# Moving the exponents ahead of two turns, and half-loads of q, in a chunked mLSTM recurrence

## The chip, the cores and the metric

The kernel runs on one core of one Trainium2 chip. The metric is the device time in microseconds of one execution. A core has five engines that run side by side, each through its own list of instructions in order: TensorE (PE) multiplies matrices and turns (transposes) tiles, its weight loads are shown as PEld; VectorE (DVE) and ScalarE (ACT) work elementwise; GpSimd (POOL) works elementwise[...]; SyncE (SP) issues transfers. TensorE writes only to PSUM, a small memory, from which VectorE or ScalarE copy. A buffer may be written again only when its last reader has ended, and this kernel fixes the order of every engine's list by the order of its source.

## What is computed

Two parts. The first is an mLSTM cell: for each of 4 batches and 8 heads, over 768 positions with 40 numbers each,

```python
for t in range(S):
    m_new  = np.maximum(f_gate[:, :, t] + m, i_gate[:, :, t])
    f_stab = np.exp(f_gate[:, :, t] + m - m_new)
    i_stab = np.exp(i_gate[:, :, t] - m_new)
    m = m_new
    C = f_stab * C + i_stab * einsum('bhd,bhe->bhde', vt, kt)
    n = f_stab * n + i_stab * kt
    h_tilde = einsum('bhde,bhe->bhd', C, qt)
    denom = np.maximum(np.abs(einsum('bhd,bhd->bh', n, qt)), 1.0)
    y[:, :, t] = sigmoid(o_gate[:, :, t]) * h_tilde / denom
```

The second takes the result as 3072 rows of 320 numbers. Each row goes by a hash of its token to one of 8 experts, `out = relu(x @ w1[e]) @ w2[e]`, with 1024 hidden numbers. The change touches the first part alone.

## The kernel before

The recurrence is done in chunks of 128 positions: 4 batches of 6 chunks are 24 steps (`NT`), step `s` being chunk `c = s % 6` of batch `b = s // 6`. Inside a chunk the recurrence is a masked, decay-weighted attention; between chunks a state C is carried. The step of the loop works on several chunks at once: it turns k for step s+2, makes the decay weights, scores and weighted scores for step s+1, attends for step s, and turns and stores the output of step s-1.

Names in the profile: `kT`, `qT` are turned k and q; `ab` the exponents' arguments, `w` the exponents (and later the weighted scores); `xb` the decay of the carried state, spread over partitions, read by `qs` (q times decay) and by `dec` (decay of the whole chunk); `ht` the output, turned, with the state's update (from `kw`) beside it in the same tile; `hT` its copy; `xo` the output turned back; `sp` scores; `R` the decay rows of a chunk; `ql` q of a whole batch as loaded, `qp` one sixth of it, padded; `og` the output gates; `tk` a small table for the experts.

```python
def load_q(b):                       # 960 KB: all heads of a batch
    qb[b] = {"l": ld.tile([P, H, NB * D], F32, name="ql", bufs=2)}
    nc.sync.dma_start(qb[b]["l"][:], q[b].rearrange("h (p r) d -> p h (r d)", r=NB))

def turn_k(s):
    d["kT"] = wk.tile([P, PR, P], F32, name="kT")
    tp = ps.tile([P, PR, P], F32, name="tr", tag="tr", bufs=2)
    for j in range(PR):              # PR = 4
        nc.tensor.transpose(tp[:, j, :], d["k"][:, 2 * j : 2 * j + 2, :]..., ident[:])
    nc.scalar.copy(d["kT"][:], tp[:])

def pad_q(b, r):
    t = qb[b][r] = qps[2 + r % 2]
    nc.vector.tensor_copy(t[:, :, :D], qb[b]["l"][:, :, r * D : (r + 1) * D])

def turn_q(b, r, cols):              # cols: every sixth position, from r
    t = qb[b].pop(r)
    tp = ps.tile([P, PR, P], F32, name="tr", tag="tr", bufs=2)
    for j in range(PR):
        nc.tensor.transpose(tp[:, j, :], t[:, 2 * j : 2 * j + 2, :]..., ident[:])
    nc.scalar.copy(qb[b]["T"][:, :, cols], tp[:])

def decays(s):
    for hf in range(2):
        ab = ps.tile([P, PR, P], F32, name="ab", bufs=2)
        for i in range(2):
            nc.tensor.matmul(ab[i * HB : (i + 1) * HB], lhsT=Ls[b % 2][...], rhs=R[:, i, hf::2, :], ...)
        nc.scalar.activation(w[:, hf], ab[:], AF.Exp)
    if c > 0:
        xb = ps.tile([P, PR, P], F32, name="xb", tag="tr", bufs=2)
        ...                          # two matmuls
        nc.vector.tensor_tensor(d["qs"][:], q_of(s), xb[:], op=ALU.mult)
        nc.scalar.copy(d["dec"][:], xb[:, :, P - 1 :])

def back(s):
    xo = d["xo"] = ps.tile([P, 2, 2, P], F32, name="xo", tag="tr", bufs=2)
    ...                              # four transposes of hT

def finish(s):                       # VectorE and GpSimd: reads xo, divides, returns the store
    ...
```

One PSUM tag, "tr", with two buffers, serves `turn_k`, `turn_q`, `back`, `xb` and `tk` in turn. The loop:

```python
turns_of = {0: (0,), 1: (1, 2), 2: (3,), 3: (4,), 4: (5,)}          # which sixths of the next batch's q
first_turns = {1: (0,), 2: (1, 2), 3: (3,), 4: (4, 5)}              # the same in batch 0
for s in range(NT):
    b, c = s // NB, s % NB
    ...                              # loads of k, v (three steps ahead)
    if c == 5 and b + 2 < B:
        load_q(b + 2)
    ...                              # output gates, a slice of expert weights
    decayed(s)
    if s + 2 < NT:
        turn_k(s + 2)
    if b == 0 and c < 4:
        turn_q0(c + 2)               # batch 0's own q, loaded by chunks
    if b + 1 < B:
        for r in (turns_of if b else first_turns).get(c, ()):
            turn_q(b + 1, r, slice(r, None, NB))
    if s > 0:
        back(s - 1)
        store = finish(s - 1)
    if s + 1 < NT:
        decays(s + 1)
    if s + 2 < NT:
        load_a(s + 2, nc.scalar if s == 0 else nc.sync)    # R
    ...
    if s > 0 and (s, "all") in og:
        sigmoid(s)                   # steps 3, 9, 15, 21; step 0's stands at the step's end
    state(s)                         # C update
    ...
    if s > 0:
        store()
    if s + 1 < NT:
        scores(s + 1)
        weigh(s + 1)
    ...                              # pad_q for the turns of the next step
    attend(s)                        # C part, then v part, then hT
    ...                              # tk and other small pieces for the experts
```

Of the kernel before, what the change touches and what calls it, by code (L numbers as in the profile page):

```python
# [8 lines left out]
F32 = mybir.dt.float32  # L9
# [8 lines left out]
P = 128  # L18
# [4 lines left out]
def kernel(  # L23
# [24 lines left out]
    nc = tc.nc  # L48
    B, H, S, D = q.shape
    BH = B * H  # L50
    NB = S // P
# [4 lines left out]
    NT = N // P  # L56
    PR = H // 2
# [47 lines left out]
    def weight_slices(e):  # L105

        W[e], slices = weights(moe_w1[e], moe_w2[e], wpools[e % 3 // 2], w2pools[2 <= e < 6])
        return slices
# [8 lines left out]
    with tc.tile_pool(name="gates", bufs=1) as gp, \  # L117
# [35 lines left out]
        qb = {}  # L153
# [5 lines left out]
        def load_k(s):  # L159
            st[s] = {"k": ks[s % NK], "v": vs[s % NK]}  # L160
            nc.sync.dma_start(ks[s % NK][:, :, :D], rows_of(k, s))

        def load_v(s):
            nc.sync.dma_start(vs[s % NK][:, :, :D], rows_of(v, s))
# [11 lines left out]
                        og[i] = tile_o[:, i - s0]  # L176
            nc.sync.dma_start(og[s], rows_of(o_gate, s))

        def load_q(b):

            qb[b] = {"l": ld.tile([P, H, NB * D], F32, name="ql", bufs=2)}
            nc.sync.dma_start(qb[b]["l"][:], q[b].rearrange("h (p r) d -> p h (r d)", r=NB))

        def load_e(b, gs):
            src = ze_d.rearrange("(g b h) i t -> b (h i) g t", g=NC2, h=H)[b]
# [5 lines left out]
        def load_a(s, eng):  # L191
            b, c = s // NB, s % NB
            r0 = c // 2 * BH + b * H
            n = 3 if c == 0 else 6
            src = za_d[r0 : r0 + H, :n, c % 2 * P : (c % 2 + 1) * P].rearrange("h i t -> i h t")
            for i in range(2):
                eng.dma_start(Rs[s % 2][32 : 32 + n, i], src)
# [59 lines left out]
        def gates_turn(rows):  # L257
            r = rows
            n = r.stop - r.start
            tp = ps.tile([P, 2, n], F32, name="tpg", tag="tr", bufs=2)  # L260
            for c in range(2):
                nc.tensor.transpose(tp[:, c, :], aP[r, c * P : (c + 1) * P], ident[r, r])
            lo, hi_ = (0, 1) if r.start == 0 else (1, 3)
            nc.vector.tensor_copy(
                kw_T[:, :, lo:hi_, :].rearrange("p c g n -> p c (g n)"), tp[:],
            )

        def turn_k(s):
            d = st[s]
# [3 lines that stand above are left out]
                nc.tensor.transpose(tp[:, j, :], d["k"][:, 2 * j : 2 * j + 2, :].rearrange("p h d -> p (h d)"), ident[:])  # L273
            nc.scalar.copy(d["kT"][:], tp[:])  # L274
# [15 lines left out]
        def load_q0(c):  # L290
            t = qb.setdefault(0, {})[c] = qps[c % 2]
            nc.sync.dma_start(t[:, :, :D], rows_of(q, c))

        def turn_q0(c):
            turn_q(0, c, slice(c * P, (c + 1) * P))

        def q_of(s):
            c = s % NB
            return qb[s // NB]["T"][:, :, c * P : (c + 1) * P]

        def decays(s):
            b, c = s // NB, s % NB
            d = st[s]
            R = Rs[s % 2]
            w = d["w"] = wk.tile([P, 2, PR, P], F32, name="w")
# [3 lines that stand above are left out]
                    nc.tensor.matmul(  # L309
                        ab[i * HB : (i + 1) * HB], lhsT=Ls[b % 2][:, c * P + i * HB : c * P + (i + 1) * HB],  # L310
                        rhs=R[:, i, hf::2, :], start=True, stop=True,
# [5 lines that stand above are left out]
                    nc.tensor.matmul(  # L317
                        xb[hf * DP : (hf + 1) * DP], lhsT=Lx[:], rhs=R[:, 0, hf::2, :], start=True, stop=True,
                    )
                d["qs"] = wk.tile([P, PR, P], F32, name="qs")  # L320
                nc.vector.tensor_tensor(d["qs"][:], q_of(s), xb[:], op=ALU.mult)
                d["dec"] = wk.tile([P, PR, 1], F32, name="dec")
                nc.scalar.copy(d["dec"][:], xb[:, :, P - 1 :])
# [89 lines left out]
        def back(s):  # L413
            d = st[s]
# [3 lines that stand above are left out]
                    nc.tensor.transpose(xo[:, hf, i, :], d["hT"][:, hf, i, :], ident[:])  # L418

        def finish(s):  # L420
            d = st.pop(s)
            hs = d["xo"].rearrange("p f i (x d) -> p f (i x) d", d=DP)
            den = wk.tile([P, 2, PR, 1], F32, name="den")
            nc.vector.tensor_scalar(
                den[:], hs[:, :, :, D:D1], scalar1=-1.0, scalar2=1.0, op0=ALU.mult, op1=ALU.max,
            )
            nc.vector.tensor_tensor(den[:], den[:], hs[:, :, :, D:D1], op=ALU.max)
            x = wk.tile([P, H, D], F32, name="x")
            xv = x.rearrange("p (j f) d -> p f j d", f=2)
            nc.vector.tensor_tensor(  # L430
                xv, hs[:, :, :, :D], og[s].rearrange("p (j f) d -> p f j d", f=2), op=ALU.mult,
            )
            nc.vector.reciprocal(den[:], den[:])  # L433
            nc.gpsimd.tensor_tensor(xv, xv, den[:].to_broadcast([P, 2, PR, D]), op=ALU.mult)  # L434
            return lambda: nc.sync.dma_start(x_d[s * P : (s + 1) * P, :], x.rearrange("p h d -> p (h d)"))
# [168 lines left out]
        after = {4: [route_counts], **{13 + i: [lambda i=i: route_table(i)] for i in range(NT // TH)}}  # L604
        after[12 + NT // TH].append(route_index)
        one = gp.tile([P, 2, 1], F32, name="one")
        turns_of = {0: (0,), 1: (1, 2), 2: (3,), 3: (4,), 4: (5,)}
        first_turns = {1: (0,), 2: (1, 2), 3: (3,), 4: (4, 5)}

        def tables():  # L610

# [76 lines left out]
        for t in vs:  # L688
            nc.gpsimd.memset(t[:, :, D1:], 0.0)
            nc.gpsimd.memset(t[:, :, D:D1], 1.0)  # L690
        load_q(1)
        gates_turn(g0)
        decays(0)
        load_a(1, A)
# [17 lines left out]
        slices = []  # L712
        for s in range(NT):
            b, c = s // NB, s % NB
            if 0 < s < NT - 3:
                load_k(s + 3)
                if b == 0 and c < 3:
                    load_q0(c + 3)
            if s + 3 < NT:
                load_v(s + 3)  # L720
            if c == 5 and b + 2 < B:
                load_q(b + 2)
            for i in range(2):
                o = s - (s - 3) % 6 + 6 + 2 * ((s - 3) % 6 - 1) + i if s > 2 else 3 + 2 * s + i
                if o < NT and (s < 3 or 1 <= (s - 3) % 6 <= 3):
                    load_o(o)
            if s in (3, 13):
                slices += weight_slices(s // 10)
            if slices:
                slices.pop(0)()  # L730
            decayed(s)
            if s + 2 < NT:
                turn_k(s + 2)
            if b == 0 and c < 4:
                turn_q0(c + 2)
            if b + 1 < B:
                for r in (turns_of if b else first_turns).get(c, ()):
                    turn_q(b + 1, r, slice(r, None, NB))
            if s > 0:
                back(s - 1)  # L740
                store = finish(s - 1)
            if s + 1 < NT:
                decays(s + 1)
            if s + 2 < NT:
                load_a(s + 2, nc.scalar if s == 0 else nc.sync)
            if s == 0:
                load_e(0, [1, 2])
            if c == 3 and b + 1 < B:
                load_e(b + 1, [0, 1, 2])
            if s > 0 and (s, "all") in og:  # L750
                sigmoid(s)
            state(s)
            if s + 1 < NT:
                k_weights(s + 1)
# [5 lines that stand above are left out]
            nb = b + (c == NB - 1)  # L760
            if nb + 1 < B and s + 1 < NT:
                for r in (turns_of if nb else first_turns).get((c + 1) % NB, ()):
                    pad_q(nb + 1, r)
            for piece in before.get(s, []):
                piece()
            attend(s)
            if s == 0:
                sigmoid(0)
                gates_turn(g1)
            for piece in after.get(s, []):  # L770
                piece()
# [92 lines left out]
    with tc.manual_schedule():  # L864
# [42 lines left out]
        for e in range(E):  # L907
# [3 lines left out]
            h = xp.tile([P, FB, CAP], F32, name="h")  # L911
# [23 lines left out]
    with tc.If(nx > 0):  # L935
        with tc.For_i(0, nx, 1) as k:
# [12 lines left out]
            h = xp.tile([P, FB, CAP], F32, name="h")  # L949
# [34 lines left out]
```

## Time and profile before

| | before |
|---|---|
| median of 3 runs | 448.51 us (447.72 to 449.46) |
| span of the profiled execution | 447.2 us |
| TensorE busy | 393.6 us (88%) |
| VectorE, ScalarE, GpSimd busy | 134.9, 136.3, 118.5 us |
| first step's kT turn / last stored row issued | 21.80 us / 187.2 us |
| one exponent (ScalarE, 48 in all) | 596 ns |
| one copy of qT (ScalarE, 24 in all), mean | 970 ns |
| one sigmoid over six chunks, and a table load | 1.80 to 1.81 us, 1.28 us |
| loads of q of a batch | 3 of 960 KB |

How to read the views. A row of the timeline gives start and length in microseconds, engine, source line, operation, tile written <- tiles read, shape and how many instructions are merged; in brackets stand the idle time before it and who ended that. Rows of one engine overlap a little, because instructions are pipelined. A row of the waits gives the engine, line and tile that waited, what it waited for, microseconds in total, how often, and the longest. A row of the windows gives the stretch, its length, the busy time of each engine with the number of instructions, the clock granted to TensorE as a share of full speed, the share of time in which the DMA engines were busy, and the rate. The chain of waits follows the work that ended last back to the start.

### The profile page before, as it was taken

How to read it: one execution, taken by the hardware profiler on the slowest of the kernel's cores; microseconds unless marked ns; L12 is line 12 of the kernel's file. 1: busy time of each engine (PE TensorE's matmuls, PEld its weight loads, DVE VectorE, ACT ScalarE, POOL GpSimd, SP SyncE). 2: the span in 40 equal slices, each digit the busy share in tenths (PEclk: the TensorE clock that was granted, in tenths of full speed). 3: DMA queues.
4: the chain of work that ended last, by engine and by line, in shares of the span. 5: the costliest groups of instructions: out<-in, count | busy, mean ns of one | idle time of the engine just before them, and what ended most of it. 6: DMA issues, size and time to landing. Idle time of an engine off the chain costs nothing.

```text
span 447.2 us, 7391 instructions
## 1 busy us (share of the span) xinstructions
PE 393.6 (88%) x2862; PEld 263.8 (59%) x2862; DVE 134.9 (30%) x371; ACT 136.3 (30%) x238; POOL 118.5 (26%) x204
## 2 busy tenths in 40 slices
PE   3367987998899999449999999999999999999993
PEld 2255766776677787325665755655656556565551
DVE  7363544575465666211112011020020110200100
ACT  5248683576358546101111111011011111101110
POOL 6363312131233343171131240311311402011011
PEclk9989997999699999959999999999999999999997
DMA  9829569559847663143751823514417200000000
GB/s 171 208 60 177 113 140 231 108 127 220 190 116 149 141 151 94 46 118 135 250 172 29 262 77 103 177 45 133 150 45 237 88 0 31 13 15 30 1 16 28
DMA packets 111736, 51.37 MB, mean 115 GB/s; under 512 B 86576, under 2 KB 105844, under 8 KB 111700
## 3 DMA queue, kind: packets, MB, share of 16 engines
q1 hardware_dynamic: 105850, 39.31, 36.1%
q0 software_dynamic: 2496, 8.20, 5.8%
q10 hardware_dynamic: 3354, 3.37, 2.3%
q8 instruction: 23, 0.38, 0.4%
q14 instruction: 13, 0.11, 0.1%
HBM read 42.00 MB, written 8.63 MB: 113 GB/s over the span
## 4 chain that ended last, share of the span: by engine, by line
PE 74%; ACT 6%; issue 6%; DMA 5%; SPq 3%; POOL 3%; DVE 1%; ACTq 0%; POOLq 0%; DVEq 0%
PE mh L825 21%; PE zp L854 20%; PE sp L345 6%; PE mh L818 6%; PE ht L403 6%; PE ab L309 3%; PE ht L396 2%; PE xo L418 2%; PE ht L376 2%; ACT kT L274 2%; SPq L101 1%; ACT hT L411 1%; ACT qT L287 1%; PE tk L582 1%; PE tp L801 1%
## 5 line engine op out<-in xcount | busy, mean ns | idle before, releaser
L854 PE MATMUL zp<-w2t,h 128*128 128x320 f32 x384 | 105.2, 433 | 0.0
L825 PE MATMUL mh<-xT,w1t 128*128 128x416 f32 x256 | 97.9, 527 | 0.9 <-issue 0.9
L854 PEld LDWEIGHTS zp<-w2t,h 128*128 128x128 f32 x384 | 72.7, 190 | 32.1 <-issue 3.3
L825 PEld LDWEIGHTS mh<-xT,w1t 128*128 128x128 f32 x256 | 47.5, 193 | 43.8 <-issue 42.7
L807 DVE COPY xT<-tp 128x384 f32<-128x384 f32 x16 | 8.9, 558 | 141.7 <-PE tp L803 124.0
L788 POOL DMA_INDIRECT out_dram<-zo,s_idx x26 | 25.6, 986 | 92.6 <-ACT zo L787 92.6
L834 ACT ACTIVATE h<-mh 128x416 f32<-128x416 f32 x32 | 16.5, 517 | 109.2 <-PE mh L818 59.6
L787 ACT COPY zo<-zp 128x320 f32<-128x320 f32 x26 | 11.1, 425 | 101.1 <-PE zp L854 92.9
L434 POOL TENSOR_TENSOR x<-x,den 128x320 f32<-128x320 f32 x24 | 17.3, 722 | 86.4 <-DVE den L433 48.3
L353 DVE TENSOR_TENSOR w<-sp,w 128x512 f32<-128x512 f32 x48 | 30.9, 686 | 19.1 <-PE sp L345 18.0
L832 DVE TENSOR_SCALAR h<-mh 128x416 f32<-128x416 f32 x32 | 18.9, 592 | 53.4 <-PE mh L825 26.9
L345 PE MATMUL sp<-qT,kT 64*128 64x128 f32 x384 | 31.6, 310 | 3.2 <-ACT qT L287 3.2
L345 PEld LDWEIGHTS sp<-qT,kT 64*128 64x128 f32 x384 | 26.5, 210 | 5.9 <-ACT qT L287 3.6
L313 ACT ACTIVATE w<-ab 128x512 f32<-128x512 f32 x48 | 26.1, 596 | 9.6 <-PE ab L309 9.1
L403 PE MATMUL ht<-w,v 128*64 128x128 f32 x384 | 28.1, 292 | 0.0
L411 ACT COPY hT<-ht 128x512 f32<-128x512 f32 x24 | 14.0, 583 | 43.8 <-PE ht L403 39.8
L818 PE MATMUL mh<-xT,w1c 64*128 64x416 f32 x128 | 26.7, 535 | 0.0
L781 POOL DMA_INDIRECT xg<-x_rows,g_idx x24 | 23.4, 975 | 9.8 <-issue 9.8
L929 POOL COPY hrem<-h 128x256 f32<-128x256 f32 x8 | 3.2, 398 | 83.2 <-ACT h L834 83.2
L403 PEld LDWEIGHTS ht<-w,v 128*64 128x64 f32 x384 | 22.0, 144 | 4.2 <-issue 3.9
L287 ACT COPY qT<-tr 128x512 f32<-128x512 f32 x24 | 22.4, 970 | 5.1 <-PE tr L286 5.1
L286 PE MATMUL tr<-ident,qp 128*128 128x128 f32 x96 | 16.3, 298 | 8.5 <-ACT kT L274 4.4
(177 smaller groups left out, 411.7 us busy)
## 6 DMA issues: line engine op xcount, KB each, us to landing
w2t<-in_moe_w_dram SPq DMA_DIRECT2D x28, 320.0 KB
w1t<-in_moe_w_dram SPq DMA_DIRECT2D x28, 256.0 KB
k<-in_k_dram SPq DMA_DIRECT2D x24, 160.0 KB
v<-in_v_dram SPq DMA_DIRECT2D x24, 160.0 KB
og<-in_o_gate_dram SPq DMA_DIRECT2D x24, 160.0 KB
x_rows<-x SPq DMA_DIRECT2D x24, 160.0 KB
ql<-in_q_dram SPq DMA_DIRECT2D x3, 960.0 KB
w1c<-in_moe_w_dram SPq DMA_DIRECT2D x14, 128.0 KB
```

The source lines that it names most:

```text
L287: nc.scalar.copy(qb[b]["T"][:, :, cols], tp[:])
L313: nc.scalar.activation(w[:, hf], ab[:], AF.Exp)
L345: nc.tensor.matmul(sp[hf][:, j, :], lhsT=d["kT"][r, j, :], rhs=q_of(s)[r, j, :], start=True, stop=True,)
L353: nc.vector.tensor_tensor(d["w"][:, hf], d["sp"][hf][:], d["w"][:, hf], op=ALU.mult)
L403: nc.tensor.matmul(place(j, hf), lhsT=d["v"][:, 2 * j + hf, :], rhs=d["w"][:, hf, j, :], start=(c == 0 and j0 == 0), stop=True, skip_group ...
L411: nc.scalar.copy(d["hT"].rearrange("p f i t -> p f (i t)"), d["ht"][:, :, : 2 * P])
L781: nc.gpsimd.indirect_dma_start(out=xg, out_offset=None, in_=x_d[:, :], in_offset=bass.IndirectOffsetOnAxis(ap=idx, axis=0),)
L788: ins = nc.gpsimd.indirect_dma_start(out=out[:, :], out_offset=bass.IndirectOffsetOnAxis(ap=idx, axis=0), in_=zo[:], in_offset=None, bound ...
L818: nc.tensor.matmul(hp[i][:, :cols], lhsT=w1c[r, fp, :], rhs=xT[r, 2, :cols], start=first, stop=not first,)
L825: nc.tensor.matmul(hp[i][:, :cols], lhsT=w1t[:, db, fb * P : (fb + 1) * P], rhs=xT[:, db, :cols], start=(first and db == 0), stop=(not fir ...
L832: nc.vector.tensor_relu(h[:, 2 * fp, :cols], hp[i][:, :cols])
L854: nc.tensor.matmul(zp[:], lhsT=h[:, fb, j * P : (j + 1) * P], rhs=w[2][:, fb, :], start=(fb == 0), stop=(fb == FB - 1),)
```

## The change

Four things. R of step s+2 is issued at the head of the step's loads. `decays(s + 1)` (ab, exponents, xb) stands right behind the turn of k, and the turn of the output and the turns of q come after it. q of the batch after next is loaded in two halves of four heads each, in chunks 2 and 4 in place of chunk 5. The turns of the next batch's q are spread one to a step, over all six chunks (in batch 0 they run over chunks 1 to 5, two of them in chunk 4). It is meant to take the large load out of the way of the small one and to let the exponents begin earlier in each step.

```diff
-        def load_q(b):
-
-            qb[b] = {"l": ld.tile([P, H, NB * D], F32, name="ql", bufs=2)}
-            nc.sync.dma_start(qb[b]["l"][:], q[b].rearrange("h (p r) d -> p h (r d)", r=NB))
+        def load_q(b, part):
+
+            if part == 0:
+                qb[b] = {"l": ld.tile([P, H, NB * D], F32, name="ql", bufs=2)}
+            hs = slice(part * PR, (part + 1) * PR)
+            nc.sync.dma_start(qb[b]["l"][:, hs], q[b, hs].rearrange("h (p r) d -> p h (r d)", r=NB))
 ...
-        turns_of = {0: (0,), 1: (1, 2), 2: (3,), 3: (4,), 4: (5,)}
-        first_turns = {1: (0,), 2: (1, 2), 3: (3,), 4: (4, 5)}
+        turns_of = {c: (c,) for c in range(NB)}
+        first_turns = {1: (0,), 2: (1,), 3: (2,), 4: (3, 4), 5: (5,)}
 ...
-        load_q(1)
+        load_q(1, 0)
+        load_q(1, 1)
 ...
         for s in range(NT):
             b, c = s // NB, s % NB
+            if 0 < s < NT - 2:
+                load_a(s + 2, nc.sync)
             if 0 < s < NT - 3:
                 load_k(s + 3)
 ...
-            if c == 5 and b + 2 < B:
-                load_q(b + 2)
+            if c in (2, 4) and b + 2 < B:
+                load_q(b + 2, c // 2 - 1)
 ...
             if s + 2 < NT:
                 turn_k(s + 2)
+            if s + 1 < NT:
+                decays(s + 1)
+            if s > 0:
+                back(s - 1)
+                store = finish(s - 1)
             if b == 0 and c < 4:
                 turn_q0(c + 2)
             if b + 1 < B:
                 for r in (turns_of if b else first_turns).get(c, ()):
                     turn_q(b + 1, r, slice(r, None, NB))
-            if s > 0:
-                back(s - 1)
-                store = finish(s - 1)
-            if s + 1 < NT:
-                decays(s + 1)
-            if s + 2 < NT:
-                load_a(s + 2, nc.scalar if s == 0 else nc.sync)
+            if s == 0:
+                load_a(s + 2, nc.scalar)
```

## The prediction

> **What bounds the kernel now.** I read first the page: the slices of the span, then the chain that ended last.
>
> ```profile
> PEclk9989997999699999959999999999999999999997
> DMA  9829569559847663143751823514417200000000
> ...
> PE 74%; ACT 6%; issue 6%; DMA 5%; SPq 3%; POOL 3%; DVE 1%; ACTq 0%; POOLq 0%; DVEq 0%
> ```
>
> TensorE carries 74% of the chain. The change touches only the recurrence (steps of the loop start at about 22 us, its last row leaves at about 187 us); the experts after it start when all rows are stored, so what the recurrence wins or loses goes into the time one for one. The granted clock is low in two slices of the recurrence's middle, the 7th and 11th (each 11.2 us), and there DMA is at 8 to 9 tenths. The table of windows holds these two places beside ordinary steps:
>
> ```profile
> core 0: us, PE busy (x) PEld busy (x) DVE busy (x) ACT busy (x) POOL busy (x), PEclk, DMA share, GB/s
> ...
> 69.00:80.20 11.20, 8.03 (x68) 6.86 (x66) 4.99 (x17) 3.46 (x6) 1.86 (x3) 0.70 0.90 201
> ...
> 87.10:93.00 5.90, 5.61 (x85) 4.46 (x83) 3.45 (x12) 3.41 (x6) 2.63 (x5) 1.00 0.47 106
> ...
> 110.30:121.00 10.70, 8.01 (x68) 6.82 (x66) 4.45 (x16) 3.46 (x6) 1.40 (x2) 0.69 1.01 225
> ```
>
> Steps 6 and 12, the first of a batch, take 11.2 and 10.7 us, though they issue fewer matmuls than step 8 (68 against 85), which takes 5.9. TensorE's waits say why, and the chain in order of time, between 96 and 123 us, who began it:
>
> ```profile
> PE tr L286 <- DVE qp L278: 2.5, 1, 2.5
> PE ab L309 <- DMA R<-decay_pieces: 1.8, 2, 1.1
> ```
>
> ```profile
> 106.20 0.58 SPq L182
> ...
> 108.66 3.13 SPq L101
> ...
> 111.84 2.84 DMA R<-decay_pieces
> ```
>
> At 106.20 the whole q of a batch (960 KB) is issued; the weights behind it hold SyncE's queue for 3.13 us, so the small decay rows R are issued only at 111.84 and land at 114.7. VectorE's copy of q waits for the load at both places too (4.8 us in two waits). Everywhere else TensorE is nearly full. Step 8 shows how a step hangs together:
>
> ```profile
> 87.08 0.65 PE L273 MATMUL tr<-ident,k 128*128 128x128 f32 x4
> ...
> 87.82 0.58 ACT L274 COPY kT<-tr 128x512 f32<-128x512 f32 x1
> ...
> 88.46 0.66 PE L418 MATMUL xo<-ident,hT 128*128 128x128 f32 x4 [0.29 <-ACT kT L274]
> ...
> 89.51 0.38 PE L317 MATMUL xb<-R,Lx 128*64 128x512 bf16 x2
> ...
> 89.53 1.08 ACT L313 ACTIVATE w<-ab 128x512 f32<-128x512 f32 x2
> ...
> 90.71 0.16 ACT L323 COPY dec<-xb 128x4 f32<-128x4 f32 x1
> ```
>
> The four users of the tag "tr" (kT, q, xo, xb) share two PSUM buffers in turn. So xo waits for the copy of kT, two allocations before: 0.29 us, the only TensorE wait of the step. The last reader of xb is dec, and dec stands on ScalarE behind both exponents.
>
> **What the skill says.** "TensorE: Matmul & The Clock Gate", Part 1: The HAM clock gate: the array falls to half clock after an idle window of about 3.4 us and needs a busy one to come back; Part 4: PE-mode transpose: transposes don't count as busy in the same way. The trace agrees: in steps 6 and 12 only transposes run for 4.8 and 4.3 us (69.1 to 73.9, 110.4 to 114.7), and the scores after them take 2.08 us instead of 1.16. But 4.5 us of the same in step 1 (33.3 to 37.8) did not bring the clock down, so it is a chance and not a threshold. "PSUM — Partial Sum Buffer", section PSUM bank collisions raise a hardware error: two engines must not touch one bank at once, not even to read. The trace agrees: dec (ScalarE) never starts before qs (VectorE), the other reader of xb, has ended. "ScalarE: Activation LUTs", section What ACT_TABLE_LOAD costs: about 1283 ns a load; here each is 1.28 us, and sigmoid (steps 0, 3, 9, 15, 21) needs one before it and the exponents one after.
>
> **The change part by part.** Steps are counted from 0; all offsets are from the start of a step's kT transposes.
>
> Loads. R two steps ahead goes to the head of SyncE's list, q of the batch after next is in SBUF three steps sooner as two halves of 480 KB (steps 2 and 4, 8 and 10). Both causes of the stall in steps 6 and 12 go: ql has over 8 us to land, R a step. Without the stall such a step would be step 8 less the product with C (0.60 us, which a batch's first step has not): 5.90 - 0.60 = 5.3. Worth 11.18 - 5.3 = 5.9 and 10.69 - 5.3 = 5.4 us, 11.3 in all. This includes the half clock: from ab to the step's end 6.3 us in each, against 0.46 + 0.22 + 0.54 + 1.09 + 1.03 = 3.3 at full clock, so 3.0 for each drop.
>
> Order of a step with one turn of q. Now, from step 8: q +0.49, xo +1.38, ab +1.97, xb +2.43, state product +2.64, end +5.90. After: ab +0.49, xb +0.95, xo still +1.38 (same wait, for the copy of kT), to +1.97. Then q takes the buffer of xb and must wait for dec: ScalarE ends kT at +1.32, the exponents (1.08) at about +2.3, and dec (0.16, with 0.1 ahead) at +2.58. So q starts at +2.64 rather than +1.97, the state product at +3.22: 0.58 us later than now. What the order saves (nothing; the wait of xo stays) is less than what it adds. That is +0.6 in each of steps 6, 8, 9, 12, 14, 15.
>
> Steps 7 and 13 turn q twice now (state product at +3.62 in step 7) and once after: -0.4 each.
>
> Last step of a batch (5, 11, 17). It has no q turn now; after, the sixth turn is there. The scores of the next batch's first step stand directly behind it and need every turn, because position t = 6p + r is spread over all six. q at +1.54, transposed at +2.2, its copy behind the exponents +2.3 to +3.35 (the strided copy takes 1.05), scores at about +3.4. Now they start at +1.61, +1.93 and +1.68: +1.8, +1.5, +1.7.
>
> Step after a sigmoid (4, 10, 16). Now in step 10: ScalarE ends sigmoid at +1.25, hT at +1.73, kT at +2.22, and only xo waits (1.18); the state product is at +3.53. After: q's copy in step 9 comes later by 0.6 and the step with it, so hT and kT end at about the same offsets (+2.28), xo at +2.34; then the table load to +3.6, exponents to +4.7, dec to +4.74, q at +4.8, state product at +5.4. That is +1.85 in steps 10 and 16. In step 4, with two turns, in the same way +6.0 against +4.49: +1.5. In step 1, which follows sigmoid 0, kT's copy ends at 36.7, table and exponents at 39.07, dec at 39.2, two turns, state product at 40.4 against 38.79: +1.6.
>
> The rest. Step 0: q waits for the copy of kT at 28.71 that xb waits for now, four transposes at half clock later: +0.65. Step 2: three turns now, two after, state product +3.80 against +4.45: -0.65. Step 3: two and two, +3.80 against +3.43: +0.4. Steps 18 to 21 turn no q: the wait for kT's copy is new to xo, about +0.1 each, 0.5 in all. Step 22: xo waits 0.85 for hT now, and has ab and xb to do first: -0.9.
>
> Sums: steps 0 to 5: 0.65 + 1.6 - 0.65 + 0.4 + 1.5 + 1.8 = +5.3. Steps 6 to 11: (-5.9 + 0.6) - 0.4 + 1.2 + 1.85 + 1.5 = -1.15. Steps 12 to 17: (-5.4 + 0.6) - 0.4 + 1.2 + 1.85 + 1.7 = -0.45. Steps 18 to 23: -0.4. In all +3.3 us: 448.5 + 3.3 = 451.8.
>
> To this comes the clock. After a sigmoid TensorE will do nothing but transposes from about +1.2 to +5.4 or +6.0 (4.2 us in steps 10 and 16, 4.8 in step 4) and about 5.6 us in step 1. Stretches of 4.3 and 4.8 us lost the clock in the trace, one of 4.5 did not. I count one drop of 3.0 us for the four places: 454.8, said as 455. This is the choice in the sum.
>
> **The rivals.** First: the stall ends and the order costs nothing (q's turn finds its buffer free, because the exponents are done while xo is turned). The 11.3 us would then come almost whole, 437 to 440. For it: this is what the order is for, and exponents start 1.2 us earlier. Against it: dec is at +2.58 by ScalarE's own durations and xo ends at +1.97; no slack is there. Second: every stretch after a sigmoid drops the clock, four times 3.0: 451.8 + 12 = 464. For it, the two drops of now; against it, step 1. Third: the load only moves; half of q, the output gates and a weight meet in steps 4 and 10, SyncE's list blocks there and k or R comes late. For it: DMA is busy 0.85 of step 10 already. Against it: R is now first, and step 4 stands at 0.59, step 8 at 0.47, so three of the four halves have room. It would give back perhaps 3 us at each place, 458 to 461.
>
> **Range and chances.** From 451.8 without any drop and some luck with the waits, to two or three drops: 447 to 462. Faster by over 2% means below 439.5 and needs the first rival: 0.04. Slower by over 2% means above 457.5, two drops or more, or the third rival: 0.26. Else within 2%.
>
> **What would show it.** Right: steps 6 and 12 near 5.9 us at clock 1.00, no wait of ab for R and none of the q copy for ql. In ordinary steps TensorE's tr L286 waits 0.6 to 0.7 us for ScalarE's dec (or VectorE's qs), a new row among the waits; in steps 5, 11 and 17 sp L345 waits over 1 us for ScalarE's qT; steps 4, 10 and 16 are 1.5 to 2 us longer than now, some at a lower clock. Wrong: if no row with dec appears, the buffers go round in another way and the first rival holds; if steps 6 or 12 still stand above 8 us, the load was not the cause.

## The result, and the profile after

| | before | changed |
|---|---|---|
| median (4 runs each) | 448.28 us | 453.87 us |
| range of the runs | 447.72 to 449.46 | 451.44 to 454.13 |
| ratio to before, 95% interval | | 1.0109 [1.0069, 1.0149] |
| span of the profiled execution | 447.2 us | 452.4 us |
| last turn of an output in the recurrence | 184.73 us | 189.27 us |

The change made the kernel slower by 1.1%. Of the 5.2 us between the two spans, 4.5 are there when the recurrence ends.

The first lines are from the page of the changed kernel: the slices of the span, and the chain that ended last by engine.

```profile
PEclk9756989998999999957999999999999999999997
DMA  8837766668846544134671632614416400000000
...
PE 74%; issue 7%; ACT 6%; DVE 5%; DMA 4%; POOL 3%; ACTq 0%; SPq 0%; POOLq 0%; DVEq 0%
```

SyncE's queue is gone from the chain (SPq 3% to 0%); VectorE (1% to 5%) has come in. The two low slices of before (the 7th and 11th) are at 9. There are new low ones at the start of the recurrence (the 2nd to 4th: 7, 5 and 6; before, 9, 8 and 9), but of these only the 4th says much: full clock stands for the first kT turn of the kernel before too, which takes 1.12 us, as in the changed one, against 0.66 later. The windows, by step of the loop:

```profile
core 0: us, PE busy (x) PEld busy (x) DVE busy (x) ACT busy (x) POOL busy (x), PEclk, DMA share, GB/s
35.00:46.70 11.70, 8.94 (x88) 6.94 (x87) 3.61 (x10) 7.28 (x10) 3.49 (x13) 0.71 0.65 122
60.50:70.40 9.90, 8.14 (x89) 5.96 (x87) 4.16 (x12) 6.38 (x9) 0.72 (x1) 0.83 0.73 165
76.90:82.70 5.80, 5.31 (x68) 3.88 (x66) 3.76 (x14) 3.39 (x6) 1.82 (x3) 1.00 0.88 186
101.90:110.90 9.00, 7.44 (x84) 5.63 (x82) 4.60 (x14) 5.35 (x8) 0.72 (x1) 0.81 0.91 201
117.00:122.80 5.80, 5.31 (x68) 3.88 (x66) 3.22 (x13) 3.39 (x6) 1.40 (x2) 1.00 0.89 195
143.90:151.50 7.60, 6.62 (x91) 5.01 (x90) 4.26 (x13) 5.28 (x9) 1.77 (x4) 1.00 0.70 147
```

These are steps 1, 4, 6, 10, 12 and 16. Steps 6 and 12, 11.2 and 10.7 us before, take 5.8 at full clock. Steps 1, 4 and 10, each behind a sigmoid, run below full clock; step 16, behind one too, does not. TensorE's waits in the changed kernel (in total, times, longest):

```profile
PE sp L347 <- ACT qT L289: 6.7, 4, 3.2
PE tr L288 <- ACT dec L325: 4.7, 11, 0.5
...
PE xo L420 <- ACT kT L276: 3.1, 3, 1.9
PE tr L288 <- DVE den L435: 2.9, 3, 1.0
```

(Lines are numbered two higher from the loads on: L288 and L289 are the turn of q and its copy.) Neither R nor ql is among them. New are q's turn behind dec, and scores behind qT (3.2 of the 6.7 us are at the start, as before). An ordinary step, step 8, in the timeline of the changed kernel:

```profile
89.17 0.66 PE L275 MATMUL tr<-ident,k 128*128 128x128 f32 x4
...
90.40 1.09 ACT L315 ACTIVATE w<-ab 128x512 f32<-128x512 f32 x2
...
90.56 0.66 PE L420 MATMUL xo<-ident,hT 128*128 128x128 f32 x4
...
91.42 0.16 ACT L325 COPY dec<-xb 128x4 f32<-128x4 f32 x1
...
91.63 0.66 PE L288 MATMUL tr<-ident,qp 128*128 128x128 f32 x4 [0.41 <-ACT dec L325]
```

The exponents do begin earlier, at +1.23 us in place of +2.45. Nothing waited for them; but dec stands behind them, and q's turn behind dec, at +2.46.

The length of each step (start of its kT turn to the next one's, us; step 4 contains 0.5 of other work), read from the timelines of six kernels:

| step | before | changed | loads alone (e1) | dec ahead (e4) | tanh (e9) | best (e10) |
|---|---|---|---|---|---|---|
| 0 | 11.66 | 13.59 | 12.31 | 13.02 | 14.45 | 11.90 |
| 1 | 8.61 | 11.71 | 8.60 | 8.75 | 7.32 | 7.33 |
| 2 | 7.70 | 6.91 | 7.71 | 6.86 | 6.92 | 7.71 |
| 3 | 6.71 | 6.92 | 6.71 | 6.87 | 6.92 | 6.71 |
| 4 | 8.21 | 10.32 | 8.22 | 7.99 | 7.39 | 7.34 |
| 5 | 4.33 | 6.07 | 4.33 | 6.07 | 6.07 | 4.33 |
| 6 | 11.18 | 5.82 | 5.31 | 5.49 | 5.83 | 5.30 |
| 7 | 6.88 | 6.44 | 7.10 | 6.45 | 6.44 | 7.22 |
| 8 | 5.90 | 6.36 | 5.90 | 5.92 | 6.36 | 5.90 |
| 10 | 6.79 | 9.04 | 6.83 | 6.49 | 6.35 | 5.90 |
| 11 | 4.65 | 6.09 | 4.66 | 6.09 | 6.10 | 4.66 |
| 12 | 10.69 | 5.83 | 5.30 | 5.39 | 5.83 | 5.58 |
| 13 | 7.59 | 7.01 | 7.81 | 6.78 | 7.01 | 7.55 |
| 16 | 6.87 | 7.57 | 6.76 | 6.60 | 7.02 | 6.57 |
| 17 | 5.08 | 6.76 | 5.08 | 6.76 | 6.77 | 5.08 |

### The profile page after: what moved, and what is told of

Same layout as the page of the kernel before. It is cut to its first block, busy times and chain, and to the rows that moved or that the text cites. A ratio compares the mean times of both kernels' runs of the same rounds, so it can differ in the third digit from the quotient of the medians.

```text
span 452.4 us, 7424 instructions
## 1 busy us (share of the span) xinstructions
PE 399.3 (88%) x2862; PEld 260.8 (58%) x2862; DVE 136.1 (30%) x371; ACT 135.4 (30%) x238; POOL 118.5 (26%) x204
## 4 chain that ended last, share of the span: by engine, by line
PE 74%; issue 7%; ACT 6%; DVE 5%; DMA 4%; POOL 3%; ACTq 0%; SPq 0%; POOLq 0%; DVEq 0%
PE mh L830 21%; PE zp L859 20%; PE sp L347 6%; PE mh L823 6%; PE ht L405 4%; PE ht L378 3%; PE ht L398 3%; PE tr L288 3%; PE tr L275 2%; PE ab L311 2%; PE tk L584 1%; ACT w L315 1%; DVE qs L323 1%; PE xo L420 1%; PE tp L806 1%
## 5 line engine op out<-in xcount | busy, mean ns | idle before, releaser
L288 PE MATMUL tr<-ident,qp 128*128 128x128 f32 x96 | 17.2, 314 | 12.3 <-ACT dec L325 4.7
L405 PE MATMUL ht<-w,v 128*64 128x128 f32 x384 | 27.1, 285 | 0.0
L289 ACT COPY qT<-tr 128x512 f32<-128x512 f32 x24 | 22.7, 958 | 8.9 <-PE tr L288 8.9
```

The lines of the kernel that those rows point to most:

```text
L405: nc.tensor.matmul(place(j, hf), lhsT=d["v"][:, 2 * j + hf, :], rhs=d["w"][:, hf, j, :], start=(c == 0 and j0 == 0), stop=True, skip_group ...
```

## The experiments

The theory: the new loads win some 11 us; the order of the step costs because dec is late; the sixth turn of q, in a batch's last step, costs because scores need it at once; and stretches behind a sigmoid lose TensorE's clock. Ratios are to the kernel before, with the 95% interval.

**e1: the loads alone.** The kernel before, with this and nothing else of the change:

```diff
+            if 0 < s < NT - 2:
+                load_a(s + 2, nc.sync)          # and no more behind decays(s + 1)
 ...
-            if c == 5 and b + 2 < B:
-                load_q(b + 2)
+            if c in (2, 4) and b + 2 < B:
+                load_q(b + 2, c // 2 - 1)       # a half of four heads
```

> The kernel before, with the loads of the change alone (R first, q in halves in chunks 2 and 4); order and turns as before. Theory (the loads win 11 us, the order and the sixth turn give back more): about 437 us, steps 6 and 12 at about 5.3 us, no lowered clock there. Rival (the stall of steps 6 and 12 has another cause, or the load only collides elsewhere): 445 us or more.

Measured: 438.87 us, 0.9796 [0.9747, 0.9846]. The page's clock and the windows of steps 6 and 12 of this kernel:

```profile
PEclk9999999999999999669999999999999999999997
```

```profile
core 0: us, PE busy (x) PEld busy (x) DVE busy (x) ACT busy (x) POOL busy (x), PEclk, DMA share, GB/s
...
68.90:74.20 5.30, 5.01 (x69) 4.08 (x66) 3.62 (x14) 3.41 (x6) 1.82 (x3) 1.00 1.02 219
104.60:110.00 5.40, 5.11 (x69) 4.14 (x68) 3.18 (x13) 3.40 (x6) 1.40 (x2) 1.00 1.01 213
```

DMA is just as busy there as before (1.02 and 1.01 of the time, against 0.90 and 1.01), and yet nothing waits: what counted was what the small rows and the copy of q stood behind, not the traffic. So about 9 us, or 2%, were in the loads, and the rest of the change gave back more than that.

**e5 and e6: which part of the loads.** e5 is the kernel before with the halves alone, R at its old place; e6 has R first and q whole in chunk 5.

```diff
 # e5
-            if c == 5 and b + 2 < B: load_q(b + 2)
+            if c in (2, 4) and b + 2 < B: load_q(b + 2, c // 2 - 1)
 # e6
+            if 0 < s < NT - 2: load_a(s + 2, nc.sync)     # and no more behind decays(s + 1)
```

> The kernel before, with q in halves in chunks 2 and 4, but R at its old place behind the bulk loads. Theory (both waits come from the 960 KB ahead of the others; R's place alone does not matter once they are gone): R is issued by about +2.5 us in step 5 and 11, a step before it is used, so nearly all is won: about 439 us, as with both. Rival (R's place is what counts): at least 443 us, ab still waits for R in steps 6 and 12.

> The kernel before, with R at the head of the loads, but q of a batch still whole and in chunk 5. Theory (the copy of q waits for its load in its own right): q's turn in steps 6 and 12 still waits 1.5 to 2.5 us, the wait of ab for R is gone (0.6 and 1.1); the steps stand at 8 to 10 us, 442 to 446 us. Rival (R's place is what counts): about 439 us.

Measured: e5 440.60 us, 0.9829 [0.9772, 0.9887], steps 6 and 12 at 5.31 and 5.30; e6 446.11 us, 0.9952 [0.9925, 0.9979], at the upper end of what was expected, those steps at 8.97 and 6.67 (step 12 below the expected 8 to 10). TensorE's waits in e6, where the copy of q still stands behind the load (`sl_i` is the next row on VectorE behind that copy):

```profile
PE tr L286 <- DVE qp L278: 2.4, 1, 2.4
...
PE tr L286 <- DVE sl_i L553: 1.3, 1, 1.3
```

Once q is out of the way R needs no better place: e5 and e1 cannot be told apart. R first alone is worth 0.5%. Whether the halves or the earlier chunks do it was not tried apart.

**e4: dec ahead of the exponents.** The changed kernel; inside `decays`, the block of xb, qs and dec is put before the loop of ab and the exponents.

```diff
 def decays(s):
+    if c > 0:
+        xb = ...; two matmuls; qs on VectorE; dec on ScalarE
     for hf in range(2):
         ab = ...; two matmuls; exponent on ScalarE
-    if c > 0:
-        xb = ...; two matmuls; qs on VectorE; dec on ScalarE
```

> The changed kernel, with xb, qs and dec made ahead of the exponents inside the same place. Theory (q's turn waits only because dec stands behind both exponents on ScalarE): the waits of tr for dec go (4.7 us in 11), steps 4, 10 and 16 win about 0.7 each and lose the clock less often: about 443 us. Rival (q's turn waits for its buffer anyway, by VectorE's reading of xo or xb): 452 to 455 us.

Measured: 442.30 us, 0.9867 [0.9822, 0.9912], so 2.4% of the kernel before lie between the changed kernel and this. TensorE's waits in it:

```profile
PE sp L347 <- ACT qT L289: 6.6, 4, 3.2
...
PE tr L288 <- DVE den L435: 1.5, 4, 0.5
...
PE tr L288 <- ACT dec L317: 0.7, 2, 0.5
```

The wait for dec falls from 4.7 us to 0.7, step 8 returns to 5.92 us, and steps 1, 4 and 10 lose 3.0, 2.3 and 2.6 us and run at full clock. The wait of scores for qT stays. The theory stands: not the order of xo and q, but the place of dec (with xb and qs) inside `decays` was the cost.

**e2: the turns as before.** The changed kernel, with the old tables of turns (none in a batch's last step, two in chunk 1).

```diff
-        turns_of = {c: (c,) for c in range(NB)}
-        first_turns = {1: (0,), 2: (1,), 3: (2,), 4: (3, 4), 5: (5,)}
+        turns_of = {0: (0,), 1: (1, 2), 2: (3,), 3: (4,), 4: (5,)}
+        first_turns = {1: (0,), 2: (1, 2), 3: (3,), 4: (4, 5)}
```

> The changed kernel, with the turns of q spread as before (none in a batch's last step). Theory (the scores wait for the copy of the sixth turn in steps 5, 11 and 17): those steps lose 1.7, 1.4 and 1.7 us, and the second turn in steps 7 and 13 costs 0.6 each: about 451 us, no wait of sp for qT. Rival (the spread of the turns is what helps, two turns in a step cost more than the wait): 455 us or more.

Measured: 448.19 us, 0.9993 [0.9963, 1.0023]. Steps 5, 11 and 17 go from 6.07, 6.09 and 6.76 to 4.42, 4.44 and 5.11 us, 1.65 less each; steps 7 and 13 grow by 0.79 and 0.61 and step 2 by 1.17. That is 2.4 us in the profiles' steps, near the 3 expected; the medians differ by more, 5.7, and the runs of this kernel are spread from 445.0 to 450.3. A part of that is the clock: in the profiled run step 4 kept it (8.84 us against 10.32).

**e3: the old order, with the loads and the spread turns.** Back and `finish` stand before `decays` again, the turns of q before both.

```diff
+            (turns of q)
+            back(s - 1); store = finish(s - 1)
             decays(s + 1)
-            back(s - 1); store = finish(s - 1)
-            (turns of q)
```

> Loads and spread turns of the change, exponents behind the two turns as before. Theory (the order is the cost): about 436 us, some 17 us below the changed kernel; in a batch's last step sp still waits for qT, but 0.5 to 0.8 us against 1.1, and no tr waits for dec. Rival (the order costs only the 4.7 us that the waits for dec show): about 448 us.

Measured: 439.11 us, 0.9787 [0.9738, 0.9837]: 15 us below the changed kernel, against 4.7 us of waits for dec. The rival falls, though the time is 3 us above the 436 expected. In the old order the sixth turn costs little (steps 5, 11 and 17 at 5.22, 5.24 and 5.91 us, 0.6 to 0.9 over before), because q's copy is ahead of the exponents on ScalarE, and no wait of scores for qT is left but the one at the start (0.5 to 0.8 us was expected in each); and single turns win in steps 7 and 13 what that costs (6.11 and 6.81 against e1's 7.10 and 7.81). e1 and e3 cannot be told apart.

**e7: dec ahead, and the turns as before.** The edits of e4 and e2 on the changed kernel together.

> The changed kernel with xb, qs and dec ahead of the exponents and the turns of q spread as before: both costs undone, the new order of xo and q kept. Theory (these two are all that the order costs beside the clock): 442.3 less 4.9 for steps 5, 11 and 17 and plus 1 to 2 for the double turns: about 438.5 us, as the loads alone. Rival (the costs overlap or something else of the order costs too): 441 us or more.

Measured: 440.81 us, 0.9818 [0.9759, 0.9876]. Between the two expectations, and not to be told from e1. With both costs undone the new order of the step is worth nothing measurable; step 8 takes 5.92 us as against 5.90. In the profiled run step 1 was at half clock for a while once more (9.73 us against e1's 8.60).

**e8 and e9: no table loads.** Both are the changed kernel with the output gate as (1 + tanh(x/2))/2. The exponent and tanh are served by one table: one table load is left in the program, in place of 11. GpSimd adds the 1; the 2 goes into the denominator.

```diff
-            nc.scalar.activation(o, o, AF.Sigmoid)
+            nc.scalar.activation(o, o, AF.Tanh, scale=0.5)
-            nc.gpsimd.memset(t[:, :, D:D1], 1.0)      # v's column for the denominator
+            nc.gpsimd.memset(t[:, :, D:D1], 2.0)
-                den[:], hs[...], scalar1=-1.0, scalar2=1.0, op0=ALU.mult, op1=ALU.max,
+                den[:], hs[...], scalar1=-1.0, scalar2=2.0, op0=ALU.mult, op1=ALU.max,
+ # e8, in sigmoid(s):       GpSimd adds 1.0 to all six chunks
+ # e9, in each step, behind store():  nc.gpsimd.tensor_scalar(og[s], og[s], scalar1=1.0, ..., op0=ALU.add)
```

> The changed kernel, with sigmoid(x) written as (1 + tanh(x/2))/2, so that exponents and gates share one table and the ten table loads of the loop go; GpSimd adds the 1, the factor 2 goes into the denominator by a column of v that holds 2 in place of 1. Theory (after a sigmoid the table load makes dec and with it q late, and TensorE then does nothing but transposes until the clock falls): steps 4, 10 and 16 fall to the length of their neighbours (7.0, 6.4 and 7.0 us), step 1 to about 8, no lowered clock after step 0: about 446 us. Rival (the lowered clock has to do with other things than these steps): steps 4 and 10 win only their stall of 0.7 us and stay near half clock: 450 us or more.

Measured: 455.19 us, 1.0157 [1.0084, 1.0230]. The time lies in the rival's range, but not for its reason: steps 4, 10 and 16 grew to 11.00, 10.45 and 9.05 us by waits that are new or longer than in the changed kernel, so this run does not decide between the two. One of TensorE's waits, and step 10 in the timeline:

```profile
PE ht L380 <- POOL kw L332: 4.5, 3, 2.0
```

```profile
98.10 5.31 POOL L341 TENSOR_SCALAR og<-og 128x320 f32<-128x320 f32 x2 [2.17 <-ACT og L339]
...
99.32 3.31 DVE L545 TENSOR_TENSOR slot<-slot,gx 128x192 f32<-128x192 f32 x1
...
103.54 0.66 PE L288 MATMUL tr<-ident,qp 128*128 128x128 f32 x4 [2.97 <-ACT dec L325]
```

GpSimd is held for 5.3 us by two additions of 1 (320 and 1600 numbers a partition), and kw, which the state product needs, stands behind them: the state product waits 2.0 us for it in steps 4 and 16. In step 10 something else came first: a row of VectorE took 3.31 us beside the larger addition, 0.36 in the kernel before, and qs, dec and q's turn stood behind it. Why that row took so long is not shown. So the addition was cut into one chunk a step.

> The changed kernel with gates by tanh once more, but GpSimd adds the 1 to one chunk in each step, behind kw of the next one, so that kw no longer waits for it. Theory (after a sigmoid the table load makes dec and with it q late, and TensorE then does nothing but transposes until the clock falls): steps 4, 10 and 16 fall to 7.0, 6.4 and 7.0 us, step 1 to about 8, no lowered clock in them: 444 to 447 us. Rival (the lowered clock comes from elsewhere): steps 4 and 10 stay above 8.3 us, 450 us or more.

Measured: 443.35 us, 0.9874 [0.9814, 0.9933], below what was expected. Steps 1, 4 and 10 in its windows:

```profile
core 0: us, PE busy (x) PEld busy (x) DVE busy (x) ACT busy (x) POOL busy (x), PEclk, DMA share, GB/s
35.00:42.30 7.30, 6.60 (x87) 4.83 (x86) 3.55 (x10) 4.46 (x8) 4.98 (x13) 1.00 0.89 167
56.20:63.60 7.40, 6.92 (x93) 5.21 (x91) 4.19 (x12) 4.64 (x8) 2.85 (x4) 1.00 0.86 197
94.60:101.00 6.40, 5.99 (x85) 4.33 (x83) 4.54 (x14) 3.33 (x6) 2.83 (x4) 1.00 0.95 199
```

Full clock in all three, 6.35 us in step 10 like its neighbours (9.04 in the changed kernel), 7.32 against 11.71 in step 1. The wait for dec in ordinary steps stays (6.2 us in 14), and so does that of scores for qT. With e4, this is two different ways to shorten the stretch behind a sigmoid, and both bring the clock back.

**e10: the best.** e1 with e9's gates.

> The loads of the change alone on the kernel before, and gates by tanh with the 1 added in the same small pieces. If the table loads cost in this order too: step 10 falls by 0.9 us, 16 by 0.2, 4 by about 1, 1 by 1.5 to 2, about 435 us against the 438.9 of the loads alone. If ScalarE has room for them: 438 to 440 us.

Measured: 435.89 us, 0.9719 [0.9660, 0.9778], faster than both kernels. The steps behind a sigmoid (1, 4, 10, 16) fall to 7.33, 7.34, 5.90 and 6.57 us, by 1.27, 0.88, 0.93 and 0.19 against e1, near the forecast in each.

## Why the prediction was right

The time (455, measured 453.87), the range and the sign were right. The sum came out as two errors that cancel, and that is luck.

**Loads: right.** Predicted 5.9 for steps 6 and 12, measured 5.82 and 5.83. e1 shows 5.3 in each without the new order, as worked out from step 8 less its product with C. The third rival, a collision of the halves in steps 4 and 10, did not occur: e1's steps 4 and 10 are 8.22 and 6.83 against 8.21 and 6.79.

**Order: the mechanism right, the size a little over.** The wait for dec was named, with 0.67 us, and the row with dec is there: 0.39 to 0.50 in each ordinary step. The step's cost is 0.46, not 0.58. The term that was too large is dec's own end: in step 8 it ended at +2.41, not +2.58, because the exponents follow kT's copy without a gap and dec follows them without the 0.1 allowed for. The first rival, that the order costs nothing, is refuted by e4.

**Last step of a batch: right.** Predicted +1.8, +1.5, +1.7; measured +1.74, +1.44, +1.68, with a wait of sp for qT of 1.15 in each. e2 takes it away.

**Step after a sigmoid: the step that failed.** The prediction said "q at +4.8, state product at +5.4. That is +1.85 in steps 10 and 16", because q takes the buffer of xb and waits for dec. Step 10 of the changed kernel, in the timeline:

```profile
104.89 0.49 DVE L432 TENSOR_TENSOR x<-xo,og 128x320 f32<-128x320 f32 x1
...
105.52 0.63 PE L288 MATMUL tr<-ident,qp 128*128 128x128 f32 x4 [0.96 <-DVE den L435]
...
106.14 0.17 ACT L325 COPY dec<-xb 128x4 f32<-128x4 f32 x1
```

q starts at +3.64, 0.6 us before dec. It cannot be in xb's buffer, which dec still reads; its wait ends with VectorE's rows on xo, and of the two buffers xo's is the one left. The two buffers of a tag do not simply alternate: in these steps the program has given q the other one. Step 16, which kept its clock, shows the cost of this place alone: +0.70 in place of +1.85.

**Clock: the place right, the reason and the count wrong.** That the stretches behind a sigmoid put the clock at risk came true, and e9 takes it away with the stretch. But the prediction measured the risk by how long only transposes run, called it a chance, and counted one drop of 3.0 us for four places. There were three in the profiled run (steps 1, 4, 10), each smaller. By the rows from the state product (step 1), the second turn of q (step 4) and the first (step 10) to the end of the step, against the same rows at full clock, they cost 1.3, 1.55 and 1.5 us, and step 1 0.8 more in its turns of q: 5.2 in all. The 3.0 was read from steps 6 and 12 of the kernel before, where half clock lasts 6.8 us; in steps 4 and 10 it lasts 3.4. What lowers it is TensorE's idle time and not the transposes (last section). So the order cost about 4.5 us less than predicted (1.1 and 1.2 in steps 10 and 16, 0.9 in step 4, 0.6 in step 1, 0.7 in the six ordinary ones), and the clock, with 0.7 more in step 0, about 3 us more.

**Steps 0 to 3.** Step 2 (-0.79) and 3 (+0.21) came as predicted (-0.65, +0.4). Of step 0 (+1.93 against +0.65) the predicted part is there: TensorE's long wait for kT's copy ends at 28.77 us in both kernels, and with q's turn behind it the state product starts at 29.81 in place of 29.02 (0.79). Of the rest, 0.41 is that the step begins earlier and waits the longer, and 0.73 is clock: the product with v takes 1.95 us in place of 1.22, because full clock is back at 34.6 and not at 32.3. The start varies so in the old order too: e1 and e6 have 12.31 and 12.93 in step 0 and 8.60 and 9.78 in step 1, though e6 differs from e1 only in loads.

## What to carry to other kernels

Before an instruction is moved ahead on one engine, look for the short ones that stand behind it in the same list and release a buffer: here a copy of 0.16 us behind two exponents of 0.6 held back a third engine at eleven places, and was worth more than what began earlier. A small load that is needed soon belongs in front of a bulk load in the same queue, or the bulk load somewhere else; the traffic itself may stay as it is. And a change of several parts should be run part by part: the loads alone were worth 2%, and were hidden in a whole that was 1% slower. To keep the clock, shorten what TensorE waits at a time: in these traces transposes kept it as well as other matmuls (last section).

## What was not expected of the hardware

The prediction let transposes count as idle; it cites the Trainium skill for that ("TensorE: Matmul & The Clock Gate", Part 4: PE-mode transpose). The traces do not agree, and they decide. In each of them the stretches of one granted clock are 3.41 us long or a multiple of it (6.83, 17.07, 20.48), so the clock changes only at points of a fixed grid. Cut at these points, the windows show what goes ahead of a change. The kernel before (twice step 1, then step 6), the changed kernel (step 1 and what follows) and e1 (step 2):

```profile
core 0: us, PE busy (x) PEld busy (x) DVE busy (x) ACT busy (x) POOL busy (x), PEclk, DMA share, GB/s
32.34:35.75 3.41, 2.31 (x26) 1.71 (x22) 1.60 (x4) 2.41 (x3) 0.46 (x1) 1.00 0.89 158
35.75:39.17 3.42, 2.29 (x29) 1.63 (x30) 0.99 (x5) 3.14 (x5) 0.29 (x1) 1.00 1.16 208
69.89:73.30 3.41, 1.06 (x8) 0.96 (x9) 1.41 (x6) 0.90 (x2) 0.00 (x0) 1.00 0.72 167
```

```profile
34.64:38.05 3.41, 1.77 (x14) 0.87 (x12) 0.98 (x2) 3.18 (x4) 0.00 (x0) 1.00 1.02 180
38.05:41.46 3.41, 2.29 (x10) 1.92 (x11) 0.84 (x4) 2.64 (x6) 1.09 (x2) 0.50 0.62 110
```

```profile
42.23:45.64 3.41, 2.46 (x20) 1.85 (x18) 0.09 (x1) 3.11 (x5) 0.41 (x1) 1.00 1.07 203
```

In the window of e1 TensorE ran nothing but transposes, for 2.46 us, and the clock stayed. In step 6 of the kernel before it was busy for 1.06 us, in step 1 of the changed one for 1.77, and half clock follows both. Over all twelve traces there are 1356 such windows at full clock: the 41 with up to 1.66 us of TensorE's time, transposes counted, were all followed by half clock; the 1308 with 1.92 us or more were not; of the seven between, four were. The time of plain matmuls alone does not part them: 1.57 us of it did not keep the clock (e8, step 4), and none at all did (e1). So a stretch of waiting costs the clock when it falls into one window. Step 1 of the kernel before had a stretch as bad, but the grid cut it in two, with 2.31 and 2.29 us busy; a window from 33.35 on would have held 1.3. Where the grid lies differs from trace to trace. That can explain the spread of e2's 12 runs, from 445.0 to 450.3 us, but only one run of each kernel has a trace, so it is not shown.

GpSimd took 1.0 us to add a constant to 128 x 320 numbers and 4.2 to 4.4 us for 128 x 1600, where its product of two tiles of 128 x 320 takes 0.72 us.
